# The last output tile in two column halves, copied by two engines and stored by two queues: where the time at the end of a kernel goes

## The chip, the cores and the metric

The kernel runs on one core of a Trainium2 chip. The metric is the device time of one execution in microseconds (us). The time before is a median of 411.13 us over the four runs that were made beside the changed kernel (410.59 to 411.77); a first three of these gave the 411.38 us that the prediction started from. A profile of one execution is the second source. Its span, first to last instruction, is about 1.8 us shorter than the time of that execution.

The change concerns the last microseconds of the run. Most of this document measures one stretch of the trace, **the tail**: from the start of the last tile's first matmul to the end of the span.

## The reference

Linformer attention (batch 8, 8 heads, 1024 tokens, head size 64, keys and values projected to 64 rows), then a feed-forward layer that takes the maximum of three up-projections (512 to 768) and projects down again (768 to 512).

```python
x = attention_out.transpose(0, 2, 1, 3).reshape(8192, 512)
h = np.maximum(np.maximum(x @ w1, x @ w2), x @ w3)
return (h @ w_out).astype(np.float32)          # 8192 x 512, float32
```

The output leaves the core as 64 tiles of 128 rows by 512 columns. Only the way in which the 64th leaves is changed.

## The kernel before

The down-projection accumulates a tile over six matmuls in one bank of PSUM, copies it to SBUF (this copy is called the evacuation below) and stores it. Tiles are stored in pairs, except in the last chunk (four tiles), where each has its own store. All output stores go through the sync engine's queue (SP).

```python
def copy(eng, o, i, ns=(), dt=0.65):
    done = {"v": nc.vector.tensor_copy, "s": nc.scalar.copy, "g": nc.gpsimd.tensor_copy}[eng](out=o, in_=i)
    ...                                        # bookkeeping for the choice of PSUM banks

def down(b, ch, tt, eng="s"):                  # one tile; tt = 0 to 3 within a chunk
    if tt % 2 == 0:
        o_sbs[0] = ffn_sb.tile([P, 2, DO], FP32, name="o_sb", bufs=3)
    o_sb = o_sbs[0]
    ov = out[b * S:(b + 1) * S, :].rearrange("(p si) m -> p si m", si=SI)
    o_ps, ns = bank()
    for jt in range(NJT):                      # NJT = 6
        nc.tensor.matmul(out=o_ps, lhsT=hTs[b, ch][:, jt, tt * P:(tt + 1) * P],
                         rhs=wout_sb[:, jt, :], start=(jt == 0), stop=(jt == NJT - 1))
        pe(MM)
    copy(eng, o_sb[:, tt % 2, :], o_ps, ns)
    run_later()
    si = ch * SPC + tt
    if b == B - 1 and ch == NCHUNK - 1:        # last chunk: one store a tile
        nc.sync.dma_start(out=ov[:, si], in_=o_sb[:, tt % 2])
    elif tt % 2:                               # else one store a pair
        nc.sync.dma_start(out=ov[:, si - 1:si + 1, :], in_=o_sb)
```

The softmax here doesn't subtract the row's maximum and nothing guards it: scores larger than these inputs give would overflow.

## Time and profile before

The page of the kernel before, its parts 1 (busy time of each engine, share of the span, instructions) and 4 (the chain of waits that ended last):

```profile
span 408.2 us, 6062 instructions
...
PE 398.7 (98%) x2438; PEld 180.1 (44%) x2438; DVE 202.6 (50%) x312; ACT 192.4 (47%) x280; POOL 32.3 (8%) x42
...
PE 92%; DMA 2%; ACT 2%; POOL 1%; DVE 1%; SPq 1%; issue 0%; DVEq 0%; ACTq 0%
```

The TensorE (PE) has no slack to speak of. The next view cuts the span at three places: the first up-projection matmul (line 506), the last one, and the first matmul of the last tile. Columns: the stretch, its length, busy time and instruction count of each engine, granted TensorE clock, busy share of the DMA engines, GB/s.

```profile
core 0: us, PE busy (x) PEld busy (x) DVE busy (x) ACT busy (x) POOL busy (x), PEclk, DMA share, GB/s
0.00:22.17 22.17, 18.41 (x164) 8.61 (x165) 8.00 (x20) 10.52 (x17) 11.31 (x18) 1.00 0.95 299
22.17:398.70 376.53, 374.75 (x2253) 169.17 (x2250) 193.59 (x291) 179.58 (x259) 20.97 (x25) 1.00 0.61 125
398.70:402.81 4.11, 4.11 (x21) 1.86 (x20) 1.01 (x2) 1.17 (x2) 0.00 (x0) 1.00 0.16 64
402.81:408.20 5.39, 1.45 (x7) 0.49 (x5) 0.00 (x0) 1.17 (x2) 0.00 (x0) 1.00 0.38 146
```

Read it by rows: a head of 22.2 us in which the DMA engines are 95% busy with the first loads; a body of 376.5 us with PE busy for all but 1.8; three tiles; and the tail, of which PE has 1.45 us of work. The tail is the only row that the change can touch. The timeline (start, length, engine, line, operation, what ended the wait before it):

```profile
402.81 1.46 PE L581 MATMUL banks<-wout_sb,hT 128*128 128x512 bf16 x6
403.01 0.59 ACT L99 COPY o_sb<-banks 128x512 f32<-128x512 f32 x1 [0.71 <-PE banks L581]
...
403.62 1.63 SPq L593 DMA_DIRECT2D out_dram<-o_sb  x2
404.30 0.59 ACT L99 COPY o_sb<-banks 128x512 f32<-128x512 f32 x1 [0.71 <-PE banks L581]
```

The two stores are shown merged; the second, the last tile's, is issued at 404.91. The DMA view of the same stretch gives their time from issue to landing, and the sync queue's own waits show what it did after that (queue, line, whom it waited for, us in total, times, longest):

```profile
out_dram<-o_sb SPq DMA_DIRECT2D x2, 256.0 KB, 2.0
```

```profile
SPq L711 <- DMA out_dram<-o_sb: 1.6, 1, 1.6
```

So the tail is a chain: six matmuls 1.46, a copy 0.59, a store 1.97, and 1.35 us of end-of-kernel waits and barriers after the landing.

### The profile page before, as it was taken

How to read it: one execution, taken by the hardware profiler on the slowest of the kernel's cores; microseconds unless marked ns; L12 is line 12 of the kernel's file. 1: busy time of each engine (PE TensorE's matmuls, PEld its weight loads, DVE VectorE, ACT ScalarE, POOL GpSimd, SP SyncE). 2: the span in 40 equal slices, each digit the busy share in tenths (PEclk: the TensorE clock that was granted, in tenths of full speed). 3: DMA queues.
4: the chain of work that ended last, by engine and by line, in shares of the span. 5: the costliest groups of instructions: out<-in, count | busy, mean ns of one | idle time of the engine just before them, and what ended most of it. 6: DMA issues, size and time to landing. Idle time of an engine off the chain costs nothing.

```text
span 408.2 us, 6062 instructions
## 1 busy us (share of the span) xinstructions
PE 398.7 (98%) x2438; PEld 180.1 (44%) x2438; DVE 202.6 (50%) x312; ACT 192.4 (47%) x280; POOL 32.3 (8%) x42
## 2 busy tenths in 40 slices
PE   7899999999999999999999999999999999999996
PEld 3444454345444544444544445444544444444442
DVE  2357664473464626636463564525465363525251
ACT  3710628623764266547445555536545556432322
POOL 0851010002000200200110002000000000000000
PEclk9999999999999999999999999999999999999999
DMA  8999979848922799598699109960420202020202
GB/s 273 343 189 207 171 169 195 200 113 124 244 46 104 129 192 254 88 226 145 199 175 193 53 4 241 205 170 0 113 95 2 103 0 104 0 104 0 104 2 103
DMA packets 58332, 54.92 MB, mean 135 GB/s; under 512 B 25920, under 2 KB 51776, under 8 KB 58304
## 3 DMA queue, kind: packets, MB, share of 16 engines
q0 software_dynamic: 25296, 25.69, 40.3%
q1 hardware_dynamic: 33008, 28.84, 21.4%
q8 instruction: 19, 0.31, 0.3%
q14 instruction: 9, 0.07, 0.1%
HBM read 57.15 MB, written 16.78 MB: 181 GB/s over the span
## 4 chain that ended last, share of the span: by engine, by line
PE 92%; DMA 2%; ACT 2%; POOL 1%; DVE 1%; SPq 1%; issue 0%; DVEq 0%; ACTq 0%
PE banks L506 61%; PE banks L581 20%; PE banks L215 4%; PE banks L276 4%; DMA k_f_93<-in_k_dram 2%; PE banks L195 2%; PE banks L287 1%; ACT pT L206 1%; POOL w_sb L171 0%; ACT zl L228 0%; POOL k_t L99 0%; DVE xT L245 0%; ACT o_sb L99 0%; POOL q_c_95 L99 0%; PE banks L371 0%
## 5 line engine op out<-in xcount | busy, mean ns | idle before, releaser
L506 PE MATMUL banks<-xT,w_sb 128*128 128x512 bf16 x1152 | 256.8, 379 | 0.0
L506 PEld LDWEIGHTS <-w_sb 128*128 128x128 bf16 x1152 | 109.7, 98 | 136.9 <-issue 9.9
L564 ACT COPY h1s<-banks 128x512 f32<-128x512 f32 x90 | 52.5, 583 | 92.9 <-PE banks L506 90.8
L581 PE MATMUL banks<-wout_sb,hT 128*128 128x512 bf16 x384 | 86.8, 379 | 0.4 <-PE banks L195 0.2
L245 DVE TENSOR_TENSOR xT<-banks,zi 128x1024 bf16<-128x1024 f32 x28 | 34.3, 1225 | 72.7 <-ACT zi L234 53.5
L99 ACT COPY o_sb<-banks 128x512 f32<-128x512 f32 x60 | 35.1, 585 | 53.7 <-PE banks L581 53.7
L581 PEld LDWEIGHTS <-hT 128*128 128x128 bf16 x384 | 36.5, 98 | 46.4 <-issue 2.9
L228 ACT ACTIVATE zl<-banks 128x1024 f32<-128x1024 f32 (+1 forms) x36 | 33.5, 931 | 29.5 <-PE banks L215 28.5
L206 ACT ACTIVATE pT<-banks 128x1024 bf16<-128x1024 f32 (+1 forms) x36 | 33.2, 931 | 14.0 <-PE banks L195 14.0
L234 ACT ACTIVATE zi<-zl 128x1024 f32<-128x1024 f32 x28 | 29.6, 1057 | 0.9
L181 POOL DMA_DIRECT2D q_t<-in_q_dram x7 | 6.1, 878 | 204.8 <-DMA qT<-q_p 146.9
L276 PEld LDWEIGHTS <-efT 128*64 128x64 bf16 x304 | 14.7, 109 | 5.7 <-issue 5.3
L195 PE MATMUL banks<-qT,kpT 64*64 64x512 bf16 (+1 forms) x144 | 13.6, 359 | 1.0 <-ACT pT L206 0.5
L215 PE MATMUL banks<-pT,ones 64*64 64x512 bf16 (+1 forms) x144 | 13.8, 375 | 0.5 <-ACT pT L206 0.3
L215 PE MATMUL banks<-pT,vp 64*64 64x512 bf16 (+1 forms) x144 | 13.2, 355 | 0.1
L371 PE MATMUL banks<-warm 128*128 128x512 bf16 x30 | 10.8, 468 | 1.2 <-DVE warm L164 1.2
L215 PEld LDWEIGHTS <-ones 64*64 64x64 bf16 x144 | 4.4, 103 | 14.5 <-issue 14.2
L99 DVE CAST vp<-banks 64x256 bf16<-64x256 f32 (+2 forms) x17 | 7.0, 410 | 7.4 <-PE banks L276 3.6
L276 PE MATMUL banks<-v_t,efT 128*64 128x256 bf16 (+1 forms) x160 | 9.6, 263 | 0.4 <-POOL v_t L99 0.4
L276 PE MATMUL banks<-k_t,efT 128*64 128x256 bf16 (+1 forms) x144 | 9.1, 263 | 0.4 <-POOL k_t L99 0.2
L99 ACT CAST vp<-banks 64x256 bf16<-64x256 f32 x14 | 5.1, 365 | 7.7 <-PE banks L276 7.5
L99 DVE COPY q_p<-q_t 128x1024 bf16<-128x1024 bf16 x24 | 8.5, 420 | 0.0
(253 smaller groups left out, 221.6 us busy)
## 6 DMA issues: line engine op xcount, KB each, us to landing
out_dram<-o_sb SPq DMA_DIRECT2D x30, 512.0 KB, 3.1
k_t<-in_k_dram POOLq DMA_DIRECT2D x7, 1024.0 KB, 14.8
q_t<-in_q_dram POOLq DMA_DIRECT2D x7, 1024.0 KB, 9.6
v_t<-in_v_dram POOLq DMA_DIRECT2D x7, 1024.0 KB, 18.9
w_sb<-in_moe_w_dram POOLq DMA_DIRECT2D x6, 384.0 KB, 6.9
k_f_92<-in_k_dram SPq DMA_DIRECT2D x1, 1024.0 KB, 7.2
k_f_93<-in_k_dram SPq DMA_DIRECT2D x1, 1024.0 KB, 9.3
v_f_96<-in_v_dram SPq DMA_DIRECT2D x1, 1024.0 KB, 12.1
```

The lines of the kernel that those rows point to most:

```text
L99: done = {"v": nc.vector.tensor_copy, "s": nc.scalar.copy, "g": nc.gpsimd.tensor_copy}[eng](out=o, in_=i)
L195: nc.tensor.matmul(out=t[c * HALF:(c + 1) * HALF, hp, 0:n * P], lhsT=kpTs[b][rows, g, :], rhs=qTs[b][rows, at:at + n, :], start=True, stop ...
L206: nc.scalar.activation(out=pTs[b, g, lo], in_=t, func=AF.Exp, scale=scale)
L215: nc.tensor.matmul(out=t[hp * HALF:(hp + 1) * HALF, c, 0:nsi * HALF], lhsT=w(rows, hp), rhs=p[rows, hp, :], start=True, stop=True,)
L228: nc.scalar.activation(out=zl, in_=t, func=AF.Ln)
L234: nc.scalar.activation(out=zi, in_=zl, func=AF.Exp, scale=-1.0)
L245: nc.vector.tensor_tensor(out=xTs[b][:, g, lo:lo + nsi, :].rearrange("a (c s) p -> a c (s p)", c=2), in0=t, in1=zi, op=ALU.mult,)
L276: nc.tensor.matmul(out=t[hh * HALF:(hh + 1) * HALF, 0:width], lhsT=efT[:, si, kv - 1, :], rhs=qkv[b][kv][:, heads[hh], si, :], start=(si = ...
L371: nc.tensor.matmul(out=t, lhsT=warm[:, 0:P], rhs=warm, start=True, stop=True)
L506: nc.tensor.matmul(out=h, lhsT=w_sb[i][:, ct, jt * P:(jt + 1) * P], rhs=xTs[b][:, ct, ch * SPC:(ch + 1) * SPC, :], start=(ct == 0), stop=( ...
L564: nc.scalar.copy(out=h1s, in_=h[0][0])
L581: nc.tensor.matmul(out=o_ps, lhsT=hTs[b, ch][:, jt, tt * P:(tt + 1) * P], rhs=wout_sb[:, jt, :], start=(jt == 0), stop=(jt == NJT - 1),)
```

## The change

The last tile's 512 columns are cut in two. Each half has its own PSUM bank, its own six matmuls of 256 columns, its own copy and store. The first half's copy and store can run while the second is computed; behind the last matmul there is then half the copy and half the bytes. The second half is copied by VectorE instead of ScalarE, and stored by ScalarE's queue instead of sync's, so that neither should have to wait for the first half.

```diff
+    def down_last(b, ch, tt):
+        si = ch * SPC + tt
+        ov = out[b * S:(b + 1) * S, :].rearrange("(p si) m -> p si m", si=SI)
+        o_sb = ffn_sb.tile([P, 2, DO], FP32, name="o_sb", bufs=3)
+        for i, (eng, queue) in enumerate((("s", nc.sync), ("v", nc.scalar))):
+            cols = slice(i * DO // 2, (i + 1) * DO // 2)
+            o_ps, ns = bank()
+            for jt in range(NJT):
+                nc.tensor.matmul(
+                    out=o_ps[:, 0:DO // 2],
+                    lhsT=hTs[b, ch][:, jt, tt * P:(tt + 1) * P],
+                    rhs=wout_sb[:, jt, cols],
+                    start=(jt == 0), stop=(jt == NJT - 1),
+                )
+                pe(MM / 2)
+            copy(eng, o_sb[:, 0, cols], o_ps[:, 0:DO // 2], ns, 0.4)
+            queue.dma_start(out=ov[:, si, cols], in_=o_sb[:, 0, cols])
+
     def down(b, ch, tt, eng="s"):
+        if b == B - 1 and ch == NCHUNK - 1 and tt == SPC - 1:
+            return down_last(b, ch, tt)
```

More of the change, by code (lines that the diff above doesn't have):

```diff
@@ L572 @@
     o_sbs = {}
+    def down_last(b, ch, tt):
[10 more added lines that the diff above has]
+                    rhs=wout_sb[:, jt, cols],
+                    start=(jt == 0),
+                    stop=(jt == NJT - 1),
+                )
+                pe(MM / 2)
+            copy(eng, o_sb[:, 0, cols], o_ps[:, 0:DO // 2], ns, 0.4)
+            queue.dma_start(out=ov[:, si, cols], in_=o_sb[:, 0, cols])
     def down(b, ch, tt, eng="s"):
+        if b == B - 1 and ch == NCHUNK - 1 and tt == SPC - 1:
+            return down_last(b, ch, tt)
         if tt % 2 == 0:
```

## The prediction

> **What bounds it now.** The page's engine table has PE busy 398.7 of 408.2 us (98%), and the chain of waits is PE for 92% of the span. The change touches nothing before the last of 64 output tiles, so only the tail can move. From the timeline and the single records of before (us from the span's start):
> - the last tile's six 128x512 matmuls start 216 ns apart; the last one ends at 404.26;
> - ScalarE copies the tile, 404.30 to 404.89 (587 ns);
> - the sync queue issues one 256 KB store at 404.91; its first packet starts at 405.75 (0.83 us later), its packets take 0.80 us (2 KB ones, 84 ns each), and its semaphore is complete at 406.88, 0.34 us after the last packet (landing view: 2.0 us from issue);
> - sync then walks through its end-of-kernel waits, about 60 ns each, and the closing barriers run to 408.2. That is 1.3 us after the landing, and fixed.
>
> So the chain from the last matmul to the end is about 4.0 us: copy 0.6, issue to landing 2.0, closing 1.3.
>
> **What the change does.**
> - PE: six 512-column matmuls become twelve of 256. Streaming is the same. The six added weight loads should hide: 128x128 transposes in this trace, each with its own weight load and only 128 columns, run 56 ns apart. Cost 0 to 0.1 us.
> - First half: its group should end near 403.62, ScalarE copies it (256-column copy, 365 ns in this trace) by 404.0, sync issues at about 404.0. Its packets queue behind the previous tile's, which end at 405.24; it lands before the second half and is off the chain.
> - Second half: PE still ends at 404.26. VectorE copies 256 float32 columns from PSUM in 417 ns (the kp group), done at 404.72, against 404.89: 0.17 us earlier. VectorE is idle here (timeline), so there is no queue in front.
> - The scalar queue issues that half at about 404.74. Packets are 1 KB; the 1 KB packets of the q loads took 46 ns against 84, so the estimate is 0.45 us of packets against 0.80. A little overlap with the first half's packets gives back about 0.1.
> - Landing: 404.74 + 0.83 + 0.5 + 0.34 = 406.4, against 406.88.
>
> [...] I credit the second queue with no bandwidth. The gain is from a shorter copy and half the bytes behind the last matmul.
>
> **On the critical path.** About 0.17 (copy) + 0.3 (packets) = 0.45 us, 0.1% of the run. Nothing upstream changes. The three runs of before spread 0.9 us, so the gain can hardly be seen in the total.
>
> **Predicted: 410.9 us, range 410.2 to 411.8. Faster by over 2%: 0.01; within 2%: 0.98; slower by over 2%: 0.01.**
>
> **What would show it.** (1) Twelve 256-column matmuls about 108 ns apart, last end near 404.3. (2) Half copies near 0.37 (ScalarE) and 0.42 us (VectorE). (3) The last store issued by ScalarE's queue near 404.75, landing in 1.6 to 1.7 us. (4) Span near 407.75, closing part still about 1.3 us.
>
> **What would make it wrong.**
> - ScalarE has issued no store before this one; its issue, or the queue's first use, may cost more than sync's 332 ns plus 0.5 us. At +0.5 us the gain is gone.
> - The two stores write interleaved rows of one output. If a wait between the queues makes the second wait for the first to land (near 406.0), the kernel gets about 1.2 us slower.
> - Weight loads that do not hide: 12 x 98 ns at most, 0.6 us more than now.
> - A longer closing sequence for another queue.

(What is cut is the ground for crediting the second queue with no bandwidth: no trace had shown it, so the credit stands as the author's estimate. No term of the sums is cut: 0.17 + 0.3 = 0.45 us of gain, and a landing at 406.4. The 0.1 us for overlapping packets is the author's guess. One expectation did not come true: the first half's packets did not queue behind the previous tile's. In the changed kernel they start at 2.289 us from the last tile's first matmul, and the previous tile's end at 2.438.)

## The result

| | runs | median us | lowest to highest |
|---|---|---|---|
| before | 4 | 411.13 | 410.59 to 411.77 |
| changed | 4 | 410.45 | 409.96 to 411.29 |

The ratio is 0.9985, with a 95% interval of 0.9962 to 1.0008. (A ratio is the mean time of one kernel's runs over that of the other's of the same rounds, so it is not quite the ratio of the two medians. Executions over 1.5% slower than the fastest of the same kernel are left out of the means.) The measured median lies in the range forecast, but the interval holds 1: the total alone does not show a gain.

The profile makes that plainer still. The profiled execution of the changed kernel has the longer span:

```profile
span 409.5 us, 6080 instructions
...
PE 398.5 (97%) x2444; PEld 180.7 (44%) x2444; DVE 203.9 (50%) x313; ACT 192.3 (47%) x280; POOL 31.9 (8%) x42
...
PE 91%; DMA 3%; ACT 2%; DVE 1%; POOL 1%; SPq 1%; issue 1%; DVEq 0%; ACTq 0%
```

The same four stretches of it, cut at the same instructions, tell where that comes from:

```profile
0.00:23.81 23.81, 18.16 (x164) 8.49 (x165) 8.91 (x20) 10.63 (x17) 10.88 (x18) 0.93 0.91 280
23.81:400.35 376.54, 374.76 (x2253) 169.25 (x2250) 193.54 (x291) 179.57 (x259) 20.99 (x25) 1.00 0.61 125
400.35:404.45 4.10, 4.10 (x20) 1.86 (x19) 1.01 (x2) 1.17 (x2) 0.00 (x0) 1.00 0.17 64
404.45:409.50 5.05, 1.47 (x13) 1.08 (x11) 0.42 (x1) 0.96 (x2) 0.00 (x0) 1.00 0.42 156
```

The head, whose code is the same, took 1.64 us longer (23.81 against 22.17). The body agrees within 0.01 us. The tail is shorter, 5.05 against 5.39 by this view's rounded cuts and 5.04 against 5.43 by the single records. A span or a total mixes a change of 0.4 us with a head that moves by more than that.

The timeline of the tail of the changed kernel:

```profile
404.78 1.15 PE L583 MATMUL banks<-wout_sb,hT 128*128 128x256 bf16 x9
...
405.70 0.36 SPq L592 DMA_DIRECT2D out_dram<-o_sb  x1
405.96 0.42 DVE L99 COPY o_sb<-banks 128x256 f32<-128x256 f32 x1 [4.50 <-DMA out_dram<-o_sb]
406.42 0.37 ACTq L592 DMA_DIRECT2D out_dram<-o_sb  x1
```

The DMA view and the sync queue's waits of the same stretch:

```profile
out_dram<-o_sb SPq DMA_DIRECT2D x1, 256.0 KB, 2.1
out_dram<-o_sb SPq DMA_DIRECT2D x1, 128.0 KB, 2.0
out_dram<-o_sb ACTq DMA_DIRECT2D x1, 128.0 KB, 1.8
```

```profile
SPq L733 <- DMA out_dram<-o_sb: 2.0, 2, 1.5
```

The second half's copy is shorter (0.42 against 0.59), its store lands 1.8 us after its issue against 2.0, and sync now waits for two landings.

One bracket in this timeline is a trap. It says that VectorE's copy waited 4.50 us for a store to land. Releasers are inferred from times. A store of an earlier tile happens to land at nearly the same moment as the last matmul ends. In every profile here the last copy starts 0.036 to 0.038 us after the last matmul's modelled end (1.458 to 1.495 in before, 1.472 to 1.510 in after); in before it started 0.011 us *ahead* of that landing. The copy waits for PE.

The single records of the tail, in us from the start of the last tile's first matmul, with the parts of the chain:

```
                               before   changed   difference of that part
last matmul ends               1.458    1.472     +0.01
last copy ends                 2.082    1.933     -0.16   (587 -> 423 ns)
last store issued              2.107    1.965     +0.01
its first packet starts        2.941    2.839     +0.04   (0.834 -> 0.874)
its last packet ends           3.738    3.338     -0.30   (0.797 -> 0.499)
its semaphore is complete      4.076    3.745     +0.07   (0.338 -> 0.407)
end of the span                5.427    5.036     -0.06   (1.351 -> 1.291)
```

The parts add up to -0.39 us. The experiments below take them apart.

### The profile page after: what moved, and what is told of

It is laid out like the page before. It is cut to its first block, busy times and chain, and to the rows that moved or that the text cites. A ratio compares the mean times of both kernels' runs of the same rounds, so it can differ in the third digit from the quotient of the medians.

```text
span 409.5 us, 6080 instructions
## 1 busy us (share of the span) xinstructions
PE 398.5 (97%) x2444; PEld 180.7 (44%) x2444; DVE 203.9 (50%) x313; ACT 192.3 (47%) x280; POOL 31.9 (8%) x42
## 4 chain that ended last, share of the span: by engine, by line
PE 91%; DMA 3%; ACT 2%; DVE 1%; POOL 1%; SPq 1%; issue 1%; DVEq 0%; ACTq 0%
PE banks L506 61%; PE banks L603 19%; PE banks L215 4%; PE banks L276 4%; DMA q_f_91<-in_q_dram 3%; PE banks L195 2%; PE banks L287 1%; ACT pT L206 1%; DMA out_dram<-o_sb 0%; POOL w_sb L171 0%; ACT zl L228 0%; POOL q_c_95 L99 0%; DVE xT L245 0%; ACT o_sb L99 0%; PE banks L371 0%
## 5 line engine op out<-in xcount | busy, mean ns | idle before, releaser
L603 PE MATMUL banks<-wout_sb,hT 128*128 128x512 bf16 x378 | 85.5, 379 | 0.4 <-PE banks L195 0.2
L99 ACT COPY o_sb<-banks 128x512 f32<-128x512 f32 (+1 forms) x60 | 34.9, 581 | 53.0 <-PE banks L603 53.0
```

## The experiments

The theory at the outset: the gain is real, and it comes from the shorter copy and the halved bytes behind the last matmul; the second engine and the second queue give nothing. Rivals: the difference between two profiles is noise; the second queue moves the tile faster; the evacuation on two engines is the whole gain. All runs computed the right result. "Landing" is when the store's semaphore is complete; times are from the start of the last tile's first matmul; the tail ends with the span.

### 1. The kernel before, profiled again (no edit)

> A second profile of the kernel before, unchanged, to see how well the tail repeats. Counted from the start of the last tile's first matmul to the end of the span, before took 5.43 us and after 5.04 us. If the tail is deterministic, this gives 5.43 within 0.03 us, and only the time up to the first up-projection matmul (22.2 us in before, 23.8 us in after) moves. If the 0.39 us gain is noise between two profiles, this can come out anywhere near 5.0 to 5.4.

Measured: tail 5.436 us, landing 4.084. The parts of the chain repeat within 0.01 us. But this execution took 414.70 us, and the four stretches show why:

```profile
0.00:26.79 26.79, 19.25 (x161) 8.44 (x165) 12.77 (x20) 10.50 (x17) 14.13 (x22) 0.87 0.99 280
26.79:403.15 376.36, 371.68 (x2211) 169.10 (x2249) 193.40 (x291) 179.56 (x259) 17.53 (x20) 1.00 0.59 123
...
407.47:412.90 5.43, 1.46 (x7) 0.49 (x5) 0.00 (x0) 1.17 (x2) 0.00 (x0) 0.85 0.37 145
```

The head took 26.79 us. In its timeline one VectorE cast took 4.94 us where it took 0.69 in the first profile of the same kernel:

```profile
16.56 4.94 DVE L99 CAST v_t<-v_f 128x1024 bf16<-128x1024 f32 x1
```

No run here tests why. It is the head that moves the total, by microseconds; the tail is deterministic to about 0.01 us.

### 2. The changed kernel, profiled and timed again (no edit)

> A second profile of the changed kernel, unchanged, and five timed rounds. Theory (tail gain real): tail 5.04 within 0.03 us, and the total 0.4 us (0.1%) under before, hardly clear of noise. Rival (noise): the tail differs from 5.04 by 0.1 us or more. The stretch from the first to the last up-projection matmul should be 376.5 us again, whatever the head does.

Measured: tail 5.039 us (5.036 before), stretch from the first to the last up-projection matmul 376.33. Timed: median 411.07 us over 6 runs (409.87 to 415.40), beside 410.86 over 11 runs of before (410.36 to 415.23); ratio 1.0004, interval 0.9955 to 1.0054. So the tail is 0.39 to 0.40 us shorter in both profiles of each kernel (5.427 and 5.436 against 5.036 and 5.039), and five timed rounds cannot see it. "Noise" falls for the tail and stands for the total.

### 3. Both stores on the sync queue

```diff
-        for i, (eng, queue) in enumerate((("s", nc.sync), ("v", nc.scalar))):
+        for i, (eng, queue) in enumerate((("s", nc.sync), ("v", nc.sync))):
```

> The changed kernel with both halves' stores issued by the sync queue. Theory (the gain is the shorter copy and the halved bytes behind the last matmul; the second queue gives nothing): sync is free when the second half is copied, so the tail stays 5.04, or is up to 0.05 us shorter because sync's first packet came 0.83 us after its issue and ScalarE's 0.87. Rival (the second queue gives the gain[...]): issue to landing goes from 1.78 back towards 1.97 us, tail near 5.2.

Measured: tail 4.996 us, landing 3.706. That is 0.04 us *shorter* than with two queues. The second half is issued at 1.963, as before, because sync had finished its first issue at 1.62; its first packet starts 0.83 us later instead of 0.87. The second queue costs 0.04 us here (one profile of each) and gives nothing.

### 4. Both copies on ScalarE

```diff
-        for i, (eng, queue) in enumerate((("s", nc.sync), ("v", nc.scalar))):
+        for i, (eng, queue) in enumerate((("s", nc.sync), ("s", nc.scalar))):
```

> The changed kernel with both half copies on ScalarE. ScalarE finishes the first half's copy at 1.23 us from the last tile's first matmul and the last matmul ends at 1.47, so it is free; its half copy took 373 ns against VectorE's 423. Theory (two engines give nothing, only the shorter copy counts): tail 0.05 us shorter, 4.99. Rival (the second engine matters): the second copy starts late and the tail grows by 0.1 us or more.

Measured: tail 4.987 us. The second copy starts at 1.510, as VectorE's did, and takes 372 ns instead of 423 to 425. The second engine costs 0.05 us.

### 5. Only the store in two halves, on two queues

The last tile keeps its six 512-column matmuls and its one ScalarE copy. (The edit is shown cut: in the run it stands in a copy of `down` for the last tile.)

```diff
-        nc.sync.dma_start(out=ov[:, si], in_=o_sb[:, tt % 2])
+        for i, queue in enumerate((nc.sync, nc.scalar)):       # last tile only
+            cols = slice(i * DO // 2, (i + 1) * DO // 2)
+            queue.dma_start(out=ov[:, si, cols], in_=o_sb[:, 0, cols])
```

> The last tile's matmuls and its one ScalarE copy as in the kernel before; only the store is cut into two column halves, one on the sync queue, one on the scalar queue. Theory ([...] the same bytes take as long, and 1 KB packets a little longer): the last packet is no earlier than before's 3.74 us from the last tile's first matmul (estimate 3.85), tail 5.4 to 5.5 us against 5.43. Rival (two queues move the tile faster): last packet near 3.4 us and tail near 5.1.

Measured: last packet at 3.781, landing 4.290, tail 5.641 us: 0.21 us *longer* than before, and longer than I expected. The two issues start 4 ns apart (2.107 and 2.111 us):

```profile
405.13 0.33 SPq L592 DMA_DIRECT2D out_dram<-o_sb  x1
405.13 0.37 ACTq L592 DMA_DIRECT2D out_dram<-o_sb  x1
```

and the DMA view shows the second landing later than the first:

```profile
out_dram<-o_sb SPq DMA_DIRECT2D x1, 128.0 KB, 2.0
out_dram<-o_sb ACTq DMA_DIRECT2D x1, 128.0 KB, 2.2
```

The packet records show where the 0.21 us arise. The last packet ends only 0.04 us later than before's (3.781 against 3.738; a 1 KB packet took 46 ns in the changed kernel's trace, so two take 92, and a 2 KB one 84); the other 0.17 us lie between that packet and the semaphore (0.51 us against 0.34). The records also show that the two stores, issued together, do not start together: the sync queue's first packet starts at 2.942, the scalar queue's at 3.194, a quarter of a microsecond more (1.08 us from its issue against 0.87 when issued alone). No run shows why. Two halves on the sync queue alone, behind one undivided copy, were not run, so what the halving costs here and what the second queue costs is not separated. The rival "two queues move a tile faster" falls.

### 6. Only matmuls and copies in two halves, one store

```diff
-            queue.dma_start(out=ov[:, si, cols], in_=o_sb[:, 0, cols])
+        nc.sync.dma_start(out=ov[:, si], in_=o_sb[:, 0])       # after both copies
```

> The last tile's matmuls and copies in two halves on ScalarE and VectorE as in the change, but one undivided 256 KB store on the sync queue after both. Theory: only the copy's part of the gain stays, issue at 1.96 us instead of 2.11, so tail 5.43 - 0.15 = 5.28 us. Rival (the evacuation on two engines is the whole gain): tail near 5.04.

Measured: tail 5.328 us, landing 3.976.

```profile
405.13 0.42 DVE L99 COPY o_sb<-banks 128x256 f32<-128x256 f32 x1 [4.50 <-DMA out_dram<-o_sb]
405.62 0.33 SPq L592 DMA_DIRECT2D out_dram<-o_sb  x1
```

```profile
out_dram<-o_sb SPq DMA_DIRECT2D x1, 256.0 KB, 2.0
```

It is 0.05 us longer than expected: the copy ends at 1.937, but sync, which here waits for two engines, issues at 2.000 and not at 1.965. The evacuation on its own is worth 0.10 us of the 0.39. The halved bytes behind it bring the landing from 3.976 to 3.745, another 0.23. This 0.23 needs the halved evacuation: halving the store alone, on two queues, made the tail longer (experiment 5).

### 7. Where the last store's semaphore stands in the closing waits

In the trace, sync ends the kernel by waiting for eight store semaphores in a fixed order, 0.06 us each even when they are long complete. The semaphores go round among the stores: the last eight of the kernel before complete on 103, 104, 105, 107, 108, 109, 118 and 101, in that order. In the kernel before, the last store's semaphore stands first of the eight, so seven waits follow its landing; the change adds one store, which moves the last one to second place, so six follow. That would be the 0.06 us by which the closing part shrank. Six more stores move it to the last place:

```diff
-        if b == B - 1 and ch == NCHUNK - 1:
+        if b == B - 1 or b == B - 2:          # 12 single stores in place of 6 paired ones
             nc.sync.dma_start(out=ov[:, si], in_=o_sb[:, tt % 2])
```

> The changed kernel, with six earlier two-tile stores issued as twelve single ones, which moves the last store's completion semaphore from the second to the last place in the row of semaphores that the sync engine waits for at the end. Theory (after the last landing the sync engine still walks the waits that stand behind it, 60 ns each; one of them less in the changed kernel is 0.06 us of its gain): landing unchanged at 3.75 us, closing part 0.92 instead of 1.29, tail 4.67 us. Rival (what I wrote before: the closing part is fixed): tail 5.04.

Measured: landing 3.741, closing part 0.923, tail 4.664 us. The records of sync's waits, changed kernel and this one (us, semaphore numbers of the stores):

```
changed:  3.224 [101]  3.762 [103]  3.826 [104]  3.888 [105]  3.947 [107]  4.009 [108]  4.068 [109]  4.130 [118]   last landing 3.745 on 103
moved:    1.735 [101]  1.797 [103]  1.861 [104]  1.923 [105]  1.982 [107]  3.018 [108]  3.218 [109]  3.758 [118]   last landing 3.741 on 118
```

Here the other waits are walked while the store is on its way. "The closing part is fixed", as I had written in the prediction, falls.

### 8. The three together

ScalarE for both copies, sync for both stores, semaphore moved.

> The changed kernel with both half copies on ScalarE, both stores on the sync queue, and the six extra stores of the run with the moved semaphore. If the three effects add up: 5.04 - 0.05 - 0.04 - 0.37 = 4.58 us. If they hide behind one another (the second half's packets can't start before the first half's end at 2.78 us), 4.63.

Measured: tail 4.585 us, landing 3.662. The effects add up within 0.01 us; the hiding that was to cost 0.05 us is not seen. (The second half's first packet starts at 2.761, 0.85 us after its issue instead of 0.83, so 0.02 us may hide.)

### 9. The kernel before, with only the semaphore moved

```diff
-        if b == B - 1 and ch == NCHUNK - 1:
+        if b >= B - 2 or (b == B - 3 and ch == NCHUNK - 1 and tt < 2):   # seven more stores
             nc.sync.dma_start(out=ov[:, si], in_=o_sb[:, tt % 2])
```

> The kernel before with its last tile whole, one engine, one store; only seven earlier two-tile stores are issued as fourteen single ones, so that the last store's semaphore stands last in the sync engine's closing waits instead of second. Theory: copy, issue and landing as in before (4.08 us), closing 0.92 instead of 1.35, tail 5.00 us: as much as the whole change (5.04), with no work of the last tile touched. Rival (the moved semaphore only helps where the halves land apart): 5.43. In the total, 0.43 us (0.1%) under before at best; I expect it not to be clear of the noise, because the time up to the first up-projection matmul moved by 4.6 us among the ten profiles so far.

(The text above says "second" because it counts a wait for other semaphores that stands ahead of the eight; among the eight it was first.) Measured: landing 4.075 as in before, closing part 0.923, tail 4.998 us. The DMA view is before's, and sync's wait for the last landing is shorter, 1.1 us against 1.6, because the walk comes ahead of it:

```profile
out_dram<-o_sb SPq DMA_DIRECT2D x1, 256.0 KB, 2.0
```

```profile
SPq L711 <- DMA out_dram<-o_sb: 1.1, 1, 1.1
```

With the last tile untouched this gains 0.43 us, slightly more than the change. Timed: 410.61 us over 6 runs beside 410.67 over 10 of before; ratio 0.9996, interval 0.9974 to 1.0018.

### 10. Three pieces instead of two

```diff
-        for i, (eng, queue) in enumerate((("s", nc.sync), ("v", nc.scalar))):
-            cols = slice(i * DO // 2, (i + 1) * DO // 2)
+        pieces = ((0, 256, "s", nc.sync), (256, 384, "v", nc.sync), (384, 512, "s", nc.scalar))
+        for c0, c1, eng, queue in pieces:
+            cols = slice(c0, c1)
```

> The changed kernel with the last tile in column pieces of 256, 128 and 128: copied by ScalarE, VectorE, ScalarE; stored by sync, sync, scalar queue. Theory (with two halves the 16 engines already move packets almost without a gap from 2.29 to 3.33 us, so a smaller last piece only queues behind the others): the last packet starts no earlier than 3.2 us, tail 4.95 to 5.15 us against 5.04. Rival (the last piece's copy and bytes are still what counts): copy 0.27 us instead of 0.42, half the packets, tail 4.7 us.

Measured: last data packet starts at 3.158, landing 3.633, tail 4.923 us. Just outside my range on the short side, far from the rival's 4.7. The last copy (128 columns, 267 ns) ends 0.14 us earlier than in the changed kernel, but its first packet starts at 2.842 against 2.839: the gain of the shorter copy is gone by then.

```profile
407.15 0.27 ACT L99 COPY o_sb<-banks 128x128 f32<-128x128 f32 x1 [0.30 <-PE banks L584]
407.45 0.37 ACTq L593 DMA_DIRECT2D out_dram<-o_sb  x1
```

The packets of the last piece took 0.35 us instead of 0.50; of these 0.15 us, 0.04 are lost again between the last packet and the semaphore (0.44 us against 0.41), and 0.11 us are gained. I had overrated how full the DMA engines were: pieces of three stores overlap in the packet records (2.29 to 2.79, 2.65 to 2.99, 2.84 to 3.19). What held the last piece's first packet back, the other piece issued 0.11 us ahead of it or the packets of the pieces before, was not separated.

### 11 and 12. The best version, timed

> The best version so far (both half copies on ScalarE, both stores on the sync queue, semaphore moved) once more, now timed. The tail should repeat at 4.58 us within 0.02, 0.85 us under before. Total: 0.2% under before if the head averages out; the interval will probably still hold 1.

The profiled execution of this run took 1444.40 us and is set aside: PE took about three times as long for the same matmuls in it (1096 ns for an up-projection matmul on average, against 379), at a granted clock that is recorded as 1.0; no run tests why. In five runs the median was 410.84 us beside 410.67 for before; ratio 1.0010, interval 0.9976 to 1.0044.

> The best version again, because its timed run's profile fell on an execution of 1444 us, in the slow state, which says nothing of the tail. Expected: tail 4.58 us within 0.02. Total: the tail's 0.85 us (0.2%) under before, but the head moves more than that between executions, so I expect a ratio between 0.996 and 1.001 with an interval that holds 1.

Measured: tail 4.586 us (4.585 in experiment 8). Five runs with a median of 409.76 us beside 411.23 over ten of before; ratio 0.9958, interval 0.9911 to 1.0005: just below the ratio that I expected, by a difference of medians (1.47 us) that is larger than the tail can give. By its tail the version is 0.84 us faster than before.

## Why the prediction was right

Its total, 410.9 us with a range of 410.2 to 411.8, held: 410.45. That total is no test of the mechanism. The range also holds the 411.13 us of the kernel before, and the two medians lie 0.68 us apart, more than the 0.39 us that the tail gives: how near the total came is in part luck. What tests the mechanism is the tail, point by point:

- **PE pays next to nothing.** Expected 0 to 0.1 us, 256-column matmuls 108 ns apart; measured 109 ns apart and 0.014 us. In the changed kernel's trace, eleven of the twelve weight loads (98 ns each) start 1 to 2 ns after a matmul does and end 9 to 10 ns before the next one starts; the twelfth ends before the first matmul.
- **The copy.** Expected 0.17 us earlier, measured 0.15 (its end; the copy itself is 164 ns shorter).
- **The packets.** Expected 0.80 to 0.5 us, measured 0.797 to 0.499. Packets of 1 KB took 46 ns, as in the first loads.
- **The second queue was credited with no bandwidth.** With both stores on sync the tail took 4.996 us, on two queues 5.039 (experiment 3); the store alone halved on two queues gave 5.641 against 5.43 undivided (experiment 5). Nor was there issuing time to save: sync's issue of the first half ended at 1.62 us, and the second half was copied at 1.93.
- **"Landing in 1.6 to 1.7 us"** was wrong; it was 1.78. Two terms were left at the sync queue's whole-tile values: 0.83 us from issue to first packet (0.87 on the scalar queue), and 0.34 us from the last packet to the semaphore (0.41). The first went with the queue: on sync it is 0.83 again (experiment 3). The difference lies in the issue itself, 0.37 us on the scalar queue and 0.33 on sync, with the first packet 0.50 us after its end on both; but sync's issue of the first half took 0.37 us too, so why is open. The second term does not go with the queue: it is 0.42 on sync too, and 0.34 to 0.35 wherever the last store is undivided (before, experiments 1, 6 and 9). Why it comes 0.07 us later stays open, but halving alone is not it: the undivided store of the tile before has 0.34 to 0.35 us from last packet to semaphore where the next store's packets start about 0.4 us or more after its own have ended (before, experiments 1, 5, 6 and 9), and 0.49 to 0.56 us where the first half's packets start before its own have ended (the changed kernel and all other experiments with a profile used here).
- **"The closing barriers … fixed"** was the step that failed. The closing part depends on where the last store's semaphore stands in the closing waits: 1.35, 1.29 or 0.92 us. This gave the change 0.06 us that I had not counted, and it made up for half of what the slower landing and the copy had lost: predicted -0.45, measured -0.33 without it and -0.39 with it.
- **"Span near 407.75"** was no test at all. It took the head for constant; among the thirteen profiles used here the head was 22.2 to 26.8 us.

Of the 0.39 us, then, 0.10 belongs to the evacuation in halves, 0.23 to the halved store behind it, and 0.06 to a semaphore that the change moved by accident. The two things its title names besides the halves, the second engine and the second queue, cost 0.05 and 0.04 us.

## What to carry to other kernels

At the end of a kernel, cut the work behind the last matmul, and leave it on whichever engine and queue is quickest for one piece: here the first engine and queue were idle again when the second half was ready, and a second one cost 0.05 and 0.04 us. (No run here shows a case in which the first is still busy.) Look at what the program does *after* the last landing as well; here a reordering of semaphores was worth as much as the whole change. And when a gain is smaller than the spread of the total, measure the stretch that the change touches, from an instruction that it doesn't touch, and repeat the profile of the unchanged kernel before you believe either.
